# The transposed input of one pair moved from a DMA transpose to TensorE, with fewer unread matmuls ahead of an earlier group

## The chip, the cores and the metric

The kernel runs on one core of a Trainium2 chip. The metric is the device time of one execution in microseconds (us); several executions are made, and their median counts. A profile of one execution gives the span (first to last instruction of the program) and every instruction in it. Engines are called PE (TensorE matmul), PEld (its weight loads), DVE (VectorE), ACT (ScalarE), POOL (GpSimd) and SP (SyncE, which issues most DMAs here); "L486" is line 486 of the kernel.

## The reference

A causal linear attention with decay, computed in blocks, is followed by a layer norm and a two-layer MLP with a residual. Batch 4, 8 heads, sequence 768, head size 64; the model width is 512, the MLP's inner width 2048.

```python
def _attn_ref(q, k, v, lam):
    B, H, S, D = q.shape            # 4, 8, 768, 64
    block = 64
    ...
    for b in range(S // block):
        qb, kb, vb = (q[:, :, sl], k[:, :, sl], v[:, :, sl])
        intra = np.einsum('bhic,bhjc->bhij', qb, kb) * Dmask[None]
        intra = np.einsum('bhij,bhjd->bhid', intra, vb)
        inter = np.einsum('bhid,bhde->bhie', qb * lam_pow[None], kv_state)
        out[:, :, sl] = intra + inter
        kv_state = lam_block * kv_state + np.einsum('bhsd,bhse->bhde', kb * rev_pow[None], vb)
    return out

def _moe_ref(x, g_ln, w_ch1, w_ch2):   # x: the attention's output, (4, 768, 512)
    mu, var = np.mean(x, -1, keepdims=True), ...
    xn = (x - mu) / np.sqrt(var + 1e-06) * g_ln
    return x + np.maximum(xn @ w_ch1, 0.0) @ w_ch2
```

## The kernel before

The work is cut into 12 windows, called u = 0 to 11: window u holds 256 positions of one batch element (three thirds of the sequence times four batch elements). A window gives two token tiles of 128 rows each, ab = 0 and 1; the two tiles of a window are a "pair", and the MLP handles one pair at a time as a "group" g, so that group g belongs to window u = g. The third group is g = 2, the fourth pair is u = 3.

For each window, the attention part does the following. SP loads q, k and v (`load_in`, L75 or L79). DVE, ACT or POOL cast and scale them into `kq` and `vb` (`in_k_one`, `in_q_one`, `in_v`). k and q are transposed into `kqT`, by PE for windows 0 to 2 and by DMA transposes on SP's queue from window 3 (`transpose_dma`, L266). PE makes the scores (`scores`, L282), DVE masks them (L292), PE makes the sums for the running state (`kv`, L316), the products with v (`av`, L428) and the inter-chunk products with the state (`inter`, L441); the last two accumulate in the PSUM banks `po0` and `po1`, one for each tile of the pair. Then `norm` copies the result to `x` on ACT (L463), takes the mean and the variance on DVE (L465, L466) and writes the centred and scaled `xc` in bf16 on DVE (L470). `rstd_of` makes the inverse deviation with a square root on ACT (L496) and a reciprocal on DVE (L498).

The MLP needs x transposed. `to_xT` makes one tile's x^T, [128, 4, 128], from `xc`. For windows 0 and 1, PE transposes four 128x128 blocks into a PSUM bank of the pool "mm" (L490) and ACT copies them to `xT` (L491). For all later windows SP issues a DMA transpose (L486).

The MLP is cut into units that are put between the steps of the attention. A unit of its first layer (`m1`, L530) is 8 matmuls of 256 columns into one "mm" bank, which ACT reads with a Relu into `hT` (L533); a group has 8 of them. A unit of the second layer (`m2`, L666) is 4 matmuls of 512 columns, and a group has 8 of them, four for each tile; after four, DVE writes the output tile (L690). From the seventh group on, the second layer is done in another way, with sums of blocks made by DVE (L548 to L550) and matmuls at L565.

PSUM has eight banks, all in use: four for "mm", two for the scores ("sc"), and `po0` and `po1`. A new tile of a tag waits until the last reader of the old one is done.

The program is written out by hand as one long list of steps; every engine runs its own instructions in the order of this list, and waits only for the data and the buffers that an instruction needs. `units(n)` takes the next n units of the MLP from a queue. Around the fourth pair the list reads: `s4(3)` (the last inter-chunk products and the norm of window 3), `to_xT(3, 0)` and `to_xT(3, 1)`, the loads of window 6 mixed with units of the third group's second layer, `rstd_of(3)`, `make_keep64()` (two masks, built on POOL, with a copy on DVE at L157), three more units, `store(2)`, the DMA transposes of window 5, and then the first unit of the fourth group.

At the first unit of the third group there is a loop of 20 unread matmuls (8 columns, from a tile of zeros; L525 and L526), written into the bank that the unit then overwrites. Each is a pair of a weight load and a matmul, and nobody reads the result:

```python
for _ in range(20 if (g, u) == (2, 0) else 0):
    nc.tensor.matmul(pm[0:8, 0, 0:8], lhsT=fill_in, rhs=fill_in, start=True, stop=True, skip_group_check=True)
```

Of the kernel before, what the change touches and what calls it, by code (L numbers as in the profile page):

```python
# [8 lines left out]
BF16 = mybir.dt.bfloat16  # L9
# [8 lines left out]
def kernel(  # L18
# [20 lines left out]
    KA = DM // 128  # L39
# [15 lines left out]
    ps = ctx.enter_context(tc.tile_pool(name="ps", bufs=1, space=PSUM))  # L55

    half = [slice(0, 64), slice(64, 128)]
    XB = 3
    LB = 6

    def mm_tile(shape, dtype, name):
        return ps.tile(shape, dtype, tag="mm", bufs=4, name=name)
# [4 lines left out]
    def source(src, u, hs):  # L67
        cc, b = divmod(u, B)
        return src[b, hs, cc * W:(cc + 1) * W, :].rearrange("h (p j) d -> p h (j d)", j=2)

    def fill(got, name, u, hs, eng=None):
        eng = eng or nc.sync
        src = dict(k=k, q=q, v=v)[name]
        if u < LB:
            eng.dma_start(got[:, hs], source(src, u, hs))  # L75
# [11 lines left out]
    def open_in(u, gate):  # L87
        qkv_in[u] = {name: inp.tile([128, H, 2 * D], F32, tag=name + "in", name=name + "in") for name in "kqv"}
        if gate:
            nc.gpsimd.memset(qkv_in[u]["k"][:, 0, 0:1], 0.0)  # L90

    def load_in(u, name, eng):
        got = qkv_in[u][name]
        fill(got, name, u, slice(0, H), eng)
        qkv_in[u][name] = got.rearrange("p h (j d) -> p h j d", j=2)
# [54 lines left out]
    def make_keep64():  # L150
        for dst, base in ((keep64, 0), (keep64_b, D)):
            nc.gpsimd.memset(dst, 1.0)
            nc.gpsimd.affine_select(
                out=dst, in_=dst, compare_op=ALU.is_ge, fill=0.0,
                base=base, pattern=[[1, D]], channel_multiplier=-1,
            )
        nc.vector.tensor_copy(keep64[half[1]], keep64_b[half[1]])  # L157
# [49 lines left out]
    def open_window(u):  # L207
        kq = wk.tile([128, 2, NP, 2, 2, D], BF16, tag="kq", bufs=3, name="kq")
        vb = wk.tile([128, H, 2, D], BF16, tag="vb", bufs=4, name="vb")
        st[u] = dict(kq=kq, vb=vb)  # L210
        if u < XB:
            st[u]["kqT"] = wk.tile([128, 2, NP, 2, 128], BF16, tag="kqT", bufs=3, name="kqT")

    def part(a, dst, hs):

        return dst[:, a, hs.start // 2:hs.stop // 2].rearrange("p a j e d -> p a e j d")
# [9 lines left out]
    def in_q(u, eng, hs=ALL):  # L226
        src = qkv_in[u]["q"][:, hs].rearrange("p (a e) j d -> p a e j d", e=2)
        dst = part(1, st[u]["kq"], hs)
        if u < LB:
            lq = lam_q[:, hs, :].rearrange("p (a e) j -> p a e j", e=2)  # L230
# [11 lines left out]
    def in_q_one(u, eng, j):  # L242
        src = qkv_in[u]["q"].rearrange("p (a e) j d -> p a e j d", e=2)
        lq = (lam_q[:, :, j] if u < LB else lam_p[:, 0, :]).rearrange("p (a e) -> p a e", e=2)
        eng.tensor_tensor(part(1, st[u]["kq"], ALL)[:, :, :, j], src[:, :, :, j],  # L245
                          lq[:, :, :, None].to_broadcast([128, NP, 2, D]), op=ALU.mult)

    def in_v(u, eng, hs=ALL):
        n = hs.stop - hs.start
        lv = lam_v[:, hs, :, None] if u < LB else lam_p[:, 1, hs, None, None]  # L250
        eng.tensor_tensor(st[u]["vb"][:, hs], qkv_in[u]["v"][:, hs], lv.to_broadcast([128, n, 2, D]), op=ALU.mult)  # L251
# [167 lines left out]
    def av(u, pairs, chunks=(0, 1)):  # L419
        s = st[u]  # L420
        if "po" not in s:
            s["po"] = [ps.tile([128, H, D], F32, tag=f"po{ab}", name=f"po{ab}") for ab in range(2)]
        for p in pairs:
            for e in range(2):
                for j in range(2):
                    for jq in range(2):
                        for ab in chunks:
                            nc.tensor.matmul(s["po"][ab][half[jq], 2 * p + e, :],  # L428
                                             lhsT=s[f"mA{p // 2}"][half[ab], e, p % 2, j, half[jq]],
                                             rhs=s["vb"][half[ab], 2 * p + e, j],  # L430
                                             start=(p == 0 and e == 0 and j == 0), stop=False, skip_group_check=True)
# [45 lines left out]
    def to_xT(u, ab):  # L477
        s = st[u]
        t = 2 * u + ab
        g = group_of[t]  # L480
        i = t - groups[g][0]
        if i == 0:
            xT_of[g] = gp.tile([128, KA, GT * 128], BF16, tag="xT", bufs=3, name="xT")
        dst = xT_of[g][:, :, i * 128:(i + 1) * 128]
        if u >= 2:
            nc.sync.dma_start_transpose(dst, s["xc"][:, ab])  # L486
        else:
            xt = mm_tile([128, KA, 128], BF16, "xt")
            for kk in range(KA):
                nc.tensor.transpose(xt[:, kk, :], s["xc"][:, ab, kk * 128:(kk + 1) * 128], ident)  # L490
            nc.scalar.copy(dst, xt)  # L491

    def rstd_of(u):
        s = st[u]
        std = wk.tile([128, 2], F32, tag="std", name="std")
        nc.scalar.activation(std, s["mv"][:, :, 1], ACT.Sqrt, bias=eps_t, scale=XS * XS)  # L496
        rstd = xp.tile([128, 2], F32, tag="rstd", name="rstd")
        nc.vector.reciprocal(rstd, std)  # L498
        x_keep[u] = (s["x"], rstd)
# [13 lines left out]
    def mlp(g):  # L513
# [6 lines left out]
        def m1(u):  # L520
            nonlocal hT
            if hT is None:
                hT = gp.tile([128, KB, GT * 128], F16, tag="hT", bufs=2, name="hT")
            pm = mm_tile([128, NB, N], F32, "pm1")
            for _ in range(20 if (g, u) == (2, 0) else 0):  # L525
                nc.tensor.matmul(pm[0:8, 0, 0:8], lhsT=fill_in, rhs=fill_in, start=True, stop=True, skip_group_check=True)  # L526
            for b in range(NB):
                n = u * NB + b
                for kk in range(KA):
                    nc.tensor.matmul(pm[:, b, :], lhsT=w1[n // W2K][:, kk, (n % W2K) * 128:(n % W2K + 1) * 128],  # L530
                                     rhs=xT_of[g][:, kk, 0:N], start=(b == 0 and kk == 0),
                                     stop=(b == NB - 1 and kk == KA - 1), skip_group_check=True)
            nc.scalar.activation(hT[:, u * NB:(u + 1) * NB, 0:N], pm, ACT.Relu)  # L533
# [138 lines left out]
        m2.sums = h_sums  # L672
        m2s[g] = m2
        return m1, m2

    def rows_of(u):

        cc, b = divmod(u, B)
        order = "(c p j) d -> j p c d" if u < LB else "(j c p) d -> j p c d"
        return out[b, cc * W:(cc + 1) * W, :].rearrange(order, c=2, j=2)  # L680
# [15 lines left out]
    def store(u):  # L696
        for j in range(2):
            nc.sync.dma_start(rows_of(u)[j], o_of[u][half[j]])
# [129 lines left out]
    def wind_up(u):  # L828


        s = st[u]
        if u < LB:
            av(u, range(NP))
# [45 lines left out]
    def s4(u):  # L879
        inter(u, 1)  # L880
        if st[u]["S"][0][1] is not None:
            norm(u, 0)
        norm(u, 1)

    def p4(u):
        to_xT(u, 0)
        to_xT(u, 1)
# [70 lines left out]
    transpose_pe(1, 0, (0, 1), nc.vector)  # L958
    transpose_pe(1, 0, (2, 3), nc.vector)
    to_xT(0, 0)  # L960
    inter(0, 1)
    norm(0, 1, early=True)
# [65 lines left out]
    def units(n):  # L1028
        for _ in range(n):
            f, *a = next(steps)  # L1030
            f(*a)
# [60 lines left out]
    s3(3)  # L1092
    units(1)
    s4(3)
    to_xT(3, 0)
    to_xT(3, 1)
    open_in(6, False)
    load_in(6, "k", nc.sync)
    units(1)
    load_in(6, "q", nc.sync)  # L1100
    units(1)
    load_in(6, "v", nc.sync)
    units(2)
    rstd_of(3)
    make_keep64()
    units(3)
    store(2)
    transpose_dma(5, 0)
# [231 lines left out]
```

## Time and profile before

| | |
|---|---|
| Median of 5 runs | 213.75 us (212.69 to 215.88; 212.79, 213.75, 214.23, 215.88, 212.69) |
| The profiled execution | 212.79 us, with a span of 211.1 us |
| Busy share of the span | PE 95%, PEld 72%, DVE 67%, ACT 46%, POOL 40% |
| First layer of the MLP, L530 on PE | 736 matmuls, 85.0 us |
| Second layer, L666 on PE | 192 matmuls, 43.3 us |
| DMA transposes xT (L486) | 20, each 1.2 to 2.8 us of SP's queue, 2.4 to 6.0 us from issue to landing |
| DMA transposes kqT (L266) | 18, each 1.2 to 2.8 us of SP's queue, 3.1 to 7.3 us to landing |
| PE transposes (L490) | 16, with 4 copies on ACT (L491) of 0.58 us |
| Unread matmuls (L526) | 20, from 54.62 us, 0.64 us in all |
| Granted TensorE clock | 1.00 |

A line of the trace in order of time gives the start, the length, the engine, the line, the operation with its output and input, how many instructions are merged into it, and in brackets the idle time before it with what ended that time. Lengths of single matmuls include the way through the array, and neighbours overlap, so the cost of a group on PE is read from its start to the start of the next. SPq is SP issuing DMAs: the length is that of the issue, not of the transfer.

### The profile page before, as it was taken

The numbers are of one execution on the slowest core, as the hardware profiler recorded it, in microseconds if no ns is written. First come the engines' busy times: TensorE is split into PE (matmuls) and PEld (weight loads), VectorE is DVE, ScalarE is ACT, GpSimd is POOL, SyncE is SP. The second block draws the span as 40 slices with busy tenths as digits, with TensorE's granted clock in tenths as the row PEclk, the third lists the DMA queues.
The fourth block names the chain that finished last, engine by engine and source line by source line (L and its number), as shares of the span: only waits on it lengthen the run. The fifth ranks groups of instructions, "written<-read, shape, count | busy, mean of one in ns | idle before, by whom it ended". The sixth has DMA issues, their size and how long they took to land.

```text
span 211.1 us, 7148 instructions
## 1 busy us (share of the span) xinstructions
PE 200.2 (95%) x3079; PEld 152.0 (72%) x3079; DVE 140.6 (67%) x293; ACT 97.5 (46%) x195; POOL 83.4 (40%) x113
## 2 busy tenths in 40 slices
PE   2988999999999999999999999999999999999992
PEld 1477788544685576487487488888888888888881
DVE  2576571459366364756997499899797887876253
ACT  3854869320254145236057067185284372661630
POOL 4647328319746083208137045265292202011020
PEclk9999999999999999999999999999999999999999
DMA  4999999999999699999979998998738850430303
GB/s 109 295 269 216 177 270 175 194 304 294 167 326 239 150 223 200 180 183 224 212 160 228 162 210 171 171 211 145 174 66 165 276 137 0 106 51 0 99 16 87
DMA packets 94305, 37.17 MB, mean 176 GB/s; under 512 B 68417, under 2 KB 91457, under 8 KB 94274
## 3 DMA queue, kind: packets, MB, share of 16 engines
q1 hardware_dynamic: 89664, 32.32, 73.4%
q0 software_dynamic: 4224, 4.19, 12.8%
q8 instruction: 24, 0.39, 0.8%
q10 hardware_dynamic: 386, 0.20, 0.4%
q14 instruction: 7, 0.06, 0.1%
HBM read 27.27 MB, written 6.29 MB: 159 GB/s over the span
## 4 chain that ended last, share of the span: by engine, by line
PE 58%; issue 13%; DVE 10%; DMA 10%; SPq 3%; POOL 3%; ACT 1%; POOLq 0%; DVEq 0%; ACTq 0%
PE pm L530 30%; PE pm L666 8%; DMA qin<-in_q_dram 5%; PE pwa L565 3%; DMA xT<-xc 3%; PE pwd L565 2%; PE pwc L565 2%; SPq L75 2%; DVE xc L470 2%; DVE stats L465 2%; DMA kqT<-kq 2%; PE po L428 2%; PE po L441 1%; PE sc L282 1%; PE pm1t L640 1%
## 5 line engine op out<-in xcount | busy, mean ns | idle before, releaser
L530 PE MATMUL pm<-xT,w 128*128 128x256 bf16 x736 | 85.0, 273 | 0.4 <-DMA xT<-xc 0.4
L530 PEld LDWEIGHTS <-w 128*128 128x128 bf16 x736 | 70.0, 98 | 10.0 <-DMA xT<-xc 0.9
L533 ACT ACTIVATE hT<-pm 128x512 f16<-128x512 f32 x92 | 55.0, 601 | 40.2 <-PE pm L530 39.4
L666 PE MATMUL pm<-w,hT 128*128 128x512 f16 x192 | 43.3, 379 | 0.0
L666 PEld LDWEIGHTS <-hT 128*128 128x128 f16 x192 | 18.2, 98 | 20.5
L322 POOL TENSOR_TENSOR Sn<-Stmp,lam_s 128x256 bf16<-128x256 f32 x16 | 9.8, 612 | 53.1 <-DVE Stmp L400 34.2
L565 PEld LDWEIGHTS <-hs 128*128 128x128 f16 x192 | 18.8, 98 | 2.2
L470 DVE SCALAR_TENSOR_TENSOR xc<-po,mv,g_row 128x512 bf16<-128x512 f32 (+1 forms) x24 | 16.8, 706 | 1.8
L292 DVE TENSOR_TENSOR mA<-sc,keep 128x512 bf16<-128x512 f32 x20 | 13.1, 684 | 7.2 <-PE sc L282 7.2
L463 ACT COPY x<-po 128x512 f32<-128x512 f32 x18 | 9.9, 589 | 16.1 <-PE po L441 10.0
L590 POOL TENSOR_TENSOR o<-ev_u,x 128x256 f32<-128x256 f32 x4 | 3.1, 784 | 31.4 <-ACT ev_u L589 31.4
L565 PEld LDWEIGHTS <-hT 128*128 128x128 f16 x144 | 13.6, 98 | 2.7 <-ACT hT L533 1.2
L465 DVE BATCH_NORM_STATS2 stats<-x 128x6 f32<-128x512 f32 x18 | 12.4, 686 | 4.0 <-ACT x L463 3.9
L548 DVE TENSOR_TENSOR hs<-hT 128x1024 f16<-128x1024 f16 x12 | 9.8, 814 | 6.8 <-ACT hT L533 6.8
L690 DVE SCALAR_TENSOR_TENSOR o<-pm,rstd,x 128x512 f32<-128x512 f32 x12 | 8.8, 744 | 7.0 <-PE pm L666 7.0
L251 POOL TENSOR_TENSOR vb<-vin,lam_p 128x1024 bf16<-128x1024 f32 x6 | 11.5, 1910 | 4.4 <-DMA vin<-in_v_dram 4.4
L245 POOL TENSOR_TENSOR kq<-qin,lam_q 128x512 bf16<-128x512 f32 x10 | 10.3, 1045 | 7.4 <-DMA qin<-in_q_dram 7.3
L251 POOL TENSOR_TENSOR vb<-vin,lam_v 128x1024 bf16<-128x1024 f32 (+1 forms) x7 | 11.8, 1687 | 2.6 <-DMA vin<-in_v_dram 2.5
L245 POOL TENSOR_TENSOR kq<-qin,lam_p 128x512 bf16<-128x512 f32 x12 | 12.3, 1043 | 0.7 <-DMA qin<-in_q_dram 0.7
L368 DVE TENSOR_TENSOR mA<-sc,keep 128x512 bf16<-128x512 f32 x12 | 8.2, 682 | 1.4 <-PE sc L362 1.4
L452 ACT COPY seen<-po 128x8 f32<-128x8 f32 x8 | 1.0, 166 | 17.5 <-PE po L441 17.5
L549 DVE TENSOR_TENSOR hs<-hs,hT 128x512 f16<-128x512 f16 x12 | 7.5, 624 | 0.4
(139 smaller groups left out, 266.8 us busy)
## 6 DMA issues: line engine op xcount, KB each, us to landing
out_dram<-o SPq DMA_DIRECT2D x18, 256.0 KB, 4.8
w<-in_moe_w_ch_dram POOLq DMA_DIRECT2D x8, 512.0 KB, 8.9
kin<-in_k_dram SPq DMA_DIRECT2D x14, 256.0 KB, 4.8
qin<-in_q_dram SPq DMA_DIRECT2D x14, 256.0 KB, 4.8
vin<-in_v_dram SPq DMA_DIRECT2D x14, 256.0 KB, 5.4
kin<-in_k_dram SPq DMA_DIRECT2D x5, 512.0 KB, 7.2
qin<-in_q_dram SPq DMA_DIRECT2D x5, 512.0 KB, 8.7
vin<-in_v_dram SPq DMA_DIRECT2D x5, 512.0 KB, 8.5
```

Source lines behind the costliest of these rows:

```text
L245: eng.tensor_tensor(part(1, st[u]["kq"], ALL)[:, :, :, j], src[:, :, :, j], lq[:, :, :, None].to_broadcast([128, NP, 2, D]), op=ALU.mult)
L251: eng.tensor_tensor(st[u]["vb"][:, hs], qkv_in[u]["v"][:, hs], lv.to_broadcast([128, n, 2, D]), op=ALU.mult)
L292: nc.vector.tensor_tensor(s[f"mA{hf}"][:, e], s[f"sc{hf}"][e], kp[:, None, :, :].to_broadcast([128, 2, 2, 128]), op=ALU.mult)
L322: eng.tensor_tensor(dst, src, lam_s[:, :, None].to_broadcast([128, NP, D]), op=ALU.mult)
L463: nc.scalar.copy(x, po)
L465: nc.vector.bn_stats(stats, po if early else x)
L470: nc.vector.scalar_tensor_tensor(xc[:, sl], in0=po[:, sl], scalar=mv[:, 0:1], in1=g_row[:, sl], op0=ALU.subtract, op1=ALU.mult)
L530: nc.tensor.matmul(pm[:, b, :], lhsT=w1[n // W2K][:, kk, (n % W2K) * 128:(n % W2K + 1) * 128], rhs=xT_of[g][:, kk, 0:N], start=(b == 0 and ...
L533: nc.scalar.activation(hT[:, u * NB:(u + 1) * NB, 0:N], pm, ACT.Relu)
L548: nc.vector.tensor_tensor(s13, b[:, :, 1:2, :].to_broadcast([128, n, 2, 128]), b[:, :, 0:4:3, :], op=ALU.subtract)
L565: nc.tensor.matmul(pr[bank], lhsT=lhs(r), rhs=rhs, start=(first and r == 0), stop=(r == KB // 2 - 1), skip_group_check=True)
L666: nc.tensor.matmul(acc[i], lhsT=hT[:, kk, i * 128:(i + 1) * 128], rhs=w2[kk // W2K][:, kk % W2K, :], start=(kk == 0), stop=(kk == KB - 1))
```

## The change

Three things are changed. The x^T of the fourth pair (u = 3 alone) is made by PE, in tiles of the tags `po0` and `po1`, and copied by ACT, where it was a DMA transpose. Its two halves stand later in the list: the first after the third of the units that follow `s4(3)`, the second after `make_keep64()`. And the loop of unread matmuls ahead of the third group runs 12 times in place of 20.

```diff
     XB = 3
+    X_PE = (3,)
     LB = 6
...
         dst = xT_of[g][:, :, i * 128:(i + 1) * 128]
-        if u >= 2:
+        if u >= 2 and u not in X_PE:
             nc.sync.dma_start_transpose(dst, s["xc"][:, ab])
         else:
-            xt = mm_tile([128, KA, 128], BF16, "xt")
+            if u < 2:
+                xt = mm_tile([128, KA, 128], BF16, "xt")
+            else:
+                xt = ps.tile([128, KA, 128], BF16, tag=f"po{ab}", name="xt")
             for kk in range(KA):
                 nc.tensor.transpose(xt[:, kk, :], s["xc"][:, ab, kk * 128:(kk + 1) * 128], ident)
             nc.scalar.copy(dst, xt)
...
-            for _ in range(20 if (g, u) == (2, 0) else 0):
+            for _ in range(12 if (g, u) == (2, 0) else 0):
...
     s4(3)
-    to_xT(3, 0)
-    to_xT(3, 1)
     open_in(6, False)
     load_in(6, "k", nc.sync)
     units(1)
     load_in(6, "q", nc.sync)
     units(1)
     load_in(6, "v", nc.sync)
-    units(2)
+    units(1)
+    to_xT(3, 0)
+    units(1)
     rstd_of(3)
     make_keep64()
+    to_xT(3, 1)
     units(3)
     store(2)
     transpose_dma(5, 0)
```

## The prediction

> **What bounds the kernel now.** I read the page's busy shares first, then the waits, then the instructions in order of time around the two edits, then SP's queue. From the page:
>
> ```profile
> PE 200.2 (95%) x3079; PEld 152.0 (72%) x3079; DVE 140.6 (67%) x293; ACT 97.5 (46%) x195; POOL 83.4 (40%) x113
> ```
>
> TensorE is busy for 95% of the span, and most of what is missing lies in the first 16 us. What an edit is worth is therefore read from PE: instructions added to it, less waits taken from it. From the waits, all that PE itself waited for after 22 us (columns: engine and line, what it waited for, us in total, times, longest):
>
> ```profile
> PE pm L530 <- DMA xT<-xc: 0.4, 2, 0.2
> ...
> PE po L441 <- DVE seen L452: 0.3, 1, 0.3
> PE sc L362 <- DMA kqT<-kq: 0.2, 1, 0.2
> ```
>
> That is 0.9 us in all, and the edits stand at the two waits of the first line: one at the third group's first matmul, one at the fourth's. PE in order of time (start, us, engine, line, operation, count, idle before it):
>
> ```profile
> 53.66 1.03 PE L666 MATMUL pm<-w,hT 128*128 128x512 f16 x4
> 54.62 0.64 PE L526 MATMUL pm<-fill_in 128*8 128x8 bf16 x20
> 55.44 3.67 PE L530 MATMUL pm<-xT,w 128*128 128x256 bf16 x32 [0.18 <-DMA xT<-xc]
> ...
> 65.72 6.22 PE L666 MATMUL pm<-w,hT 128*128 128x512 f16 x28
> 72.14 1.03 PE L530 MATMUL pm<-xT,w 128*128 128x256 bf16 x8 [0.20 <-DMA xT<-xc]
> ```
>
> The reader is to see how little stands free: after the 28 matmuls of L666, which are the seven units that cover the way of the fourth pair's x^T, PE waits 0.2 us; after the 20 unread matmuls of L526 it waits 0.18 us. SP's queue over the same time:
>
> ```profile
> 62.65 4.80 SPq L266 DMA_TRANSPOSE kqT<-kq  x2
> 67.55 3.19 SPq L486 DMA_TRANSPOSE xT<-xc  x2
> 70.79 1.20 SPq L79 DMA_DIRECT2D kin<-in_k_dram  x2
> ...
> 82.32 1.21 SPq L79 DMA_DIRECT2D kin<-in_k_dram  x2
> 83.65 3.79 SPq L486 DMA_TRANSPOSE xT<-xc  x2
> ```
>
> SP hardly rests: each transfer starts when the one before it has been issued.
>
> **The x^T of the fourth pair: what it removes.** Two DMA transposes leave SP (3.19 us of its queue), and PE's wait for them goes. How long that wait is: 32 matmuls of L666 elsewhere run from 98.63 to the next group at 105.63; every change of group costs about 0.10 (four of them, 0.87 in a stream, take 65.48 - 64.51 = 0.97 before another group), so one is (7.00 - 0.10)/32 = 0.2156. 28 of them and the seam are 6.14: PE would be free at 71.86, and began at 72.14. Saved: 0.28 us.
>
> **What it adds.** Eight PE transposes, in two fours between units of L666. The kernel does the same for its first pairs, and these rows price it:
>
> ```profile
> 28.31 0.39 PE L490 MATMUL xt<-ident,xc 128*128 128x128 bf16 x4
> 28.53 1.04 PE L530 MATMUL pm<-xT,w 128*128 128x256 bf16 x8
> 29.75 0.40 PE L490 MATMUL xt<-ident,xc 128*128 128x128 bf16 x4 [0.18 <-DVE xc L470]
> ```
>
> Start to start, four take 28.53 - 28.31 = 0.22. In the stream of L666 each four opens one more seam: 0.22 + 0.10 = 0.32, two fours 0.64. Lower end 0.22 each (no extra seam), 0.44; upper end 0.40 + 0.10 each (the row that began after a wait), 1.0. I take 0.64, the row without a wait, since both operands are there: xc's halves are ready at 66.83 and 68.50 (DVE L470 at 66.08 and 67.75, 0.75 each), and the fours come up after 12 matmuls at 65.72 + 12 x 0.2156 + 0.10 = 68.41 and, four more on, at 69.59.
>
> A rule speaks against this edit. The Trainium skill's page "TensorE: Matmul & The Clock Gate", section "Part 4: PE-mode transpose", puts one 128x128 transpose at about 275 ns within a kernel, and says that transposes don't count as activity for the clock gate. The rows have single transposes of 219 to 314 ns from start to end, but pipelined, 55 ns apart; by the page's figure taken in series the estimate would be 8 x 0.275 = 2.2 us more, 215.7. The rows decide.
>
> Two ACT copies from the bank to xT (L491, 0.58 each). ACT is empty there, with one square root at 67.74 and then 5.23 us of idle until 73.27; the copies would run at about 68.85 and 70.05 (0.43 after their transposes start, by 29.75 to 30.18), and the second ends at 70.6. The group needs them when PE has done the last 12 matmuls, at 69.81 + 2.69 = 72.5. Cover 1.9 us; were it gone, the 0.28 would not be saved. Behind the first copy stands the square root, now at 69.4 instead of 67.74, and behind it DVE's reciprocal and the copy for keep64, at 69.7 instead of 69.2: DVE has nothing from 69.5 to 71.98, and the reciprocal's first reader comes at 85.4. No cost.
>
> The banks po0 and po1 are free once xc and x are read, which the transposes need anyway; their next writer is the fifth pair's L428 at 78.10, 7 us later. No cost.
>
> **What moves on SP.** The loads of the seventh window, the store and the kqT transposes behind them start 3.2 us earlier. The gain ends at 83.65, where the next x^T transposes wait for DVE's xc, done at 82.87 + 0.75 = 83.62, and that is paced by PE. Between, POOL waits less for v (2.13 us at 81.12) and ACT less for k (2.46 at 87.28), both off PE's path. So 0; lower end -0.35, if emptier DMA engines also remove the 0.21 before L362 at 122.47 and its like.
>
> **The unread matmuls.** 20 start at 54.62 and take 0.64 us, 32 ns each; eight fewer end 0.26 earlier. But PE then stood 0.18 us for the xT transpose, which nothing of this change moves. The wait becomes 0.44: worth 0; lower end -0.26, if that transfer lands before the 12 end.
>
> **The sum.** -0.28 + 0.64 + 0 + 0 = +0.36 us. Lower end -0.28 + 0.44 - 0.35 - 0.26 = -0.45, upper -0.28 + 1.0 = +0.72. The profiled execution took 212.79 us, a span of 211.1 and 1.69 around it; it becomes 213.15. It is one of the fast ones among the five runs: their median lies 0.96 above it. On the median the sum gives 213.75 + 0.36 = 214.1. The five runs spread from 212.69 to 215.88, so about 1% is what a measurement of this kernel tells from no change.
>
> **Rivals.** (1) *Somewhat faster: the wait removed is larger in most executions than in the profiled one.* For it: x^T transposes land 2.4 to 6.0 us after issue, the fourth pair's in 3.8 at most, and PE has no reserve there; a landing of 6.0 would cost PE over 2 us. If all of the median's 0.96 were that wait, 213.75 + 0.36 - 0.96 = 213.15; with both lower ends (-0.35, -0.26) 212.5. Against it: nothing shows that the slower runs lose their time there, and later transposes have the same risk.
>
> (2) *Slower, by the clock.* The unread matmuls and the steady stream keep PE at pace. Early in the kernel it runs at half: 16 matmuls of 128 columns at 16.47 take 18.13 - 16.47 = 1.66 us, 104 ns each, against 56 ns (32 in 1.79) from 30.14:
>
> ```profile
> 16.47 1.87 PE L640 MATMUL pm1t<-xT,w 128*128 128x128 bf16 x16 [0.32 <-ACT xT L491]
> 18.13 0.63 PE L490 MATMUL xt<-ident,xc 128*128 128x128 bf16 x4
> ...
> 20.09 1.38 PE L640 MATMUL pm1t<-xT,w 128*128 128x128 bf16 x16
> 21.41 0.42 PE L282 MATMUL sc<-kqT 64*64 64x128 bf16 x16
> ```
>
> The last 16 take 1.32, so the pace turned near 21.0. A relapse of that length, 4.5 us at half pace, loses 2.25: 216.35. It decides once the gap ahead of the third group is long enough to drop the pace; the longest gaps after 22 us, up to 0.28, did not, and the change makes one of 0.44. Against it: 0.44 is short, and the page's granted clock is 9 tenths or more in every slice. That row does not show the early half pace either, so pace, not the clock row, has to be looked at.
>
> (3) *Slower, by a collision.* The early loads of the seventh window share the engines with the kqT transposes that SP issued at 62.65 to 67.45, whose last lands 5.3 after 65.53, at 70.8; the fifth pair's scores read them at 73.38. If one load, 3.7 us to landing, got ahead, PE would wait 70.8 + 3.7 - 73.4 = 1.1: 214.1 + 1.1 = 215.2. It decides from 2.6 us of delay on. Against it: one queue, and the transposes stand ahead in it.
>
> (4) *It doesn't do what it says:* ACT's copies come too late and PE waits as before. By the cover of 1.9 us that is unlikely; it would give +0.64 at least, 214.4.
>
> **How the numbers follow.** Forecast 0.55, (1) 0.25, (2) 0.05, (3) 0.08, (4) 0.07. The likeliest is 214.1. The range reaches down to (1) with its lower ends, 212.5, and up to the collision on top of the upper end, 213.75 + 0.72 + 1.1 = 215.6; the clock case lies outside. Under 211.6 (1% faster) no case lands, only a median of few runs drawn low: 0.05. Over 215.9 lie the clock case and an unlucky draw: 0.09. Within 1%: 0.86.
>
> **What would show it.** Right: the group of L486 at 67.55 gone; L490 in two fours near 68.4 and 69.6, 0.22 to 0.4 each; no idle time before L530 near 72.5; the loads of the seventh window issued from about 67.5; 12 of L526 with some 0.44 us of idle behind them; every later stage 0.3 to 0.4 us later; SP again waiting for xc near 84. Wrong: the fourth group's first matmul before 72.0 or after 73; matmuls of 256 columns at twice their pace after 55; an idle PE before the fifth pair's scores; or a median outside the spread of the runs before.

## The result and the profile after

The changed kernel takes 212.92 us at the median of 53 runs (211.52 to 215.76), the kernel before 213.80 us at the median of 95 (211.22 to 217.09). The ratio, from runs of both on the same chip, is 0.9985, with a 95% interval of 0.997 to 1.0001: -0.3 us, -0.6 to 0, which is no difference that these runs can tell from nothing. Most of the 0.88 us between the two medians therefore comes from the chips and the runs that are pooled in them. Executions over 1.5% slower than the fastest of their kernel are left out of the ratios, and one profile, that of "SP's queue as before", is of such an execution. The profiled execution took 211.95 us with a span of 210.2, against 212.79 and 211.1 before.

The page, first part, of the changed kernel:

```profile
PE 199.4 (95%) x3079; PEld 151.5 (72%) x3079; DVE 139.9 (67%) x293; ACT 98.5 (47%) x197; POOL 83.0 (39%) x113
```

The number of matmuls is the same as before, 3079: eight transposes came, eight unread matmuls went. That plays a part below. In the waits of PE no line with a DMA into xT is left; of those after 22 us that the prediction showed, one remains:

```profile
PE po L442 <- DVE seen L453: 0.3, 1, 0.3
```

PE in order of time, around both edits (lines that stood at L530 and L666 are now L534 and L670; those between the diff's first line and `to_xT` are 1 higher):

```profile
54.00 0.45 PE L530 MATMUL pm<-fill_in 128*8 128x8 bf16 x12
54.38 3.67 PE L534 MATMUL pm<-xT,w 128*128 128x256 bf16 x32
...
64.72 2.76 PE L670 MATMUL pm<-w,hT 128*128 128x512 f16 x12
67.32 0.39 PE L494 MATMUL xt<-ident,xc 128*128 128x128 bf16 x4
67.54 1.03 PE L670 MATMUL pm<-w,hT 128*128 128x512 f16 x4
68.41 0.39 PE L494 MATMUL xt<-ident,xc 128*128 128x128 bf16 x4
68.63 2.75 PE L670 MATMUL pm<-w,hT 128*128 128x512 f16 x12
71.22 1.04 PE L534 MATMUL pm<-xT,w 128*128 128x256 bf16 x8
```

Each four of transposes takes 0.22 us from its start to the next line's, and nothing is idle in front of either group (the third at 54.38, the fourth at 71.22). SP's queue:

```profile
61.73 4.49 SPq L267 DMA_TRANSPOSE kqT<-kq  x2
66.26 2.00 SPq L80 DMA_DIRECT2D kin<-in_k_dram  x2
...
79.32 1.21 SPq L80 DMA_DIRECT2D kin<-in_k_dram  x2
82.77 2.86 SPq L487 DMA_TRANSPOSE xT<-xc  x2
```

The loads come right behind the kqT transposes, and from 80.53 to 82.77 SP waits for xc: the relief of the queue ends there.

The span is best read in three stages, because whole executions differ by more than the change can be worth. S3 runs from the first of the 36 second-layer matmuls of L666 to the third group's first matmul, S4 from the first of the 28 to the fourth group's first, and "rest" from there to the end. Every number is a difference of two starts in PE's order of time.

| kernel | 36 matmuls begin at | S3 | S4 | rest |
|---|---|---|---|---|
| before | 46.74 | 8.70 | 6.42 | 138.96 |
| changed | 46.12 | 8.26 | 6.50 | 138.98 |
| 12 unread, x^T by DMA | 48.53 | 8.32 | 6.55 | 139.22 |
| 20 unread, x^T by PE | 46.02 | 8.45 | 6.50 | 139.75 |
| none unread, x^T by DMA | 47.95 | 8.23 | 6.06 | 140.80 |
| the same again | 47.46 | 8.74 | 6.06 | 140.58 |
| none unread, x^T by PE | 46.82 | 8.06 | 6.50 | 139.96 |
| third pair on PE too, none unread | 46.03 | 8.23 | 6.50 | 140.18 |
| the same again | 46.30 | 8.23 | 6.50 | 139.50 |
| third pair on PE too, 4 unread | 46.13 | 8.50 | 6.50 | 139.19 |

Of the 0.9 us between the two profiled spans, 0.62 lie ahead of 46, where the two kernels do the same work; S3 gives 0.44, the stretch between S3 and S4 (10.28 against 10.34), S4 and the rest take back 0.06, 0.08 and 0.02.

### The profile page after: what moved, and what is told of

It reads as the page before. It is cut to its first block, busy times and chain, and to the rows that moved or that the text cites. A ratio compares the mean times of both kernels' runs of the same rounds, so it can differ in the third digit from the quotient of the medians.

```text
span 210.2 us, 7143 instructions
## 1 busy us (share of the span) xinstructions
PE 199.4 (95%) x3079; PEld 151.5 (72%) x3079; DVE 139.9 (67%) x293; ACT 98.5 (47%) x197; POOL 83.0 (39%) x113
## 4 chain that ended last, share of the span: by engine, by line
PE 62%; issue 13%; DMA 12%; DVE 5%; POOL 3%; SPq 2%; ACT 1%; POOLq 0%; DVEq 0%; ACTq 0%
PE pm L534 28%; PE pm L670 17%; DMA w<-in_moe_w_ch_dram 5%; DMA qin<-in_q_dram 4%; PE pwa L569 3%; DMA kin<-in_k_dram 3%; PE pwc L569 3%; PE pwd L569 2%; SPq L76 2%; PE po L442 2%; PE sc L283 1%; PE pwb L569 1%; PE po L429 1%; POOL o L594 1%; POOL kq L246 1%
## 5 line engine op out<-in xcount | busy, mean ns | idle before, releaser
L534 PE MATMUL pm<-xT,w 128*128 128x256 bf16 x736 | 85.0, 273 | 0.0
L534 PEld LDWEIGHTS <-w 128*128 128x128 bf16 x736 | 70.0, 98 | 9.3
L670 PE MATMUL pm<-w,hT 128*128 128x512 f16 x192 | 43.6, 379 | 0.0
L670 PEld LDWEIGHTS <-hT 128*128 128x128 f16 x192 | 18.1, 98 | 20.1
L569 PEld LDWEIGHTS <-hs 128*128 128x128 f16 x192 | 18.7, 98 | 2.5 <-DVE hs L552 0.3
L569 PEld LDWEIGHTS <-hT 128*128 128x128 f16 x144 | 13.6, 98 | 2.7 <-ACT hT L537 1.2
L552 DVE TENSOR_TENSOR hs<-hT 128x1024 f16<-128x1024 f16 x12 | 10.6, 884 | 6.9 <-ACT hT L537 6.9
L442 PE MATMUL po<-Sn,kqT 64*64 64x64 bf16 x216 | 7.5, 199 | 0.3 <-DVE seen L453 0.3
```

Of the source, the lines that this page charges most:

```text
L442: nc.tensor.matmul(s["po"][ab][half[jq], 2 * p + e, :], lhsT=qT[half[e], p, jq, half[ab]], rhs=s["S"][ab][jq][half[e], p, :], start=False, ...
L552: nc.vector.tensor_tensor(s13, b[:, :, 1:2, :].to_broadcast([128, n, 2, 128]), b[:, :, 0:4:3, :], op=ALU.subtract)
L569: nc.tensor.matmul(pr[bank], lhsT=lhs(r), rhs=rhs, start=(first and r == 0), stop=(r == KB // 2 - 1), skip_group_check=True)
L670: nc.tensor.matmul(acc[i], lhsT=hT[:, kk, i * 128:(i + 1) * 128], rhs=w2[kk // W2K][:, kk % W2K, :], start=(kk == 0), stop=(kk == KB - 1))
```

## The experiments

**One part of the change at a time.** Only the count of the loop:

```diff
-            for _ in range(20 if (g, u) == (2, 0) else 0):
+            for _ in range(12 if (g, u) == (2, 0) else 0):
```

> Only the loop of unread matmuls is changed (12 in place of 20); the x^T of the fourth pair stays a DMA transpose. Theory A (the unread matmuls stood on PE's path, because the third group's x^T has landed by then in many executions): 8 x 0.032 = 0.26 us less where it has landed, nothing where it has not; time -0.26 to 0 us, and in the profile no idle time or less than 0.44 us ahead of the third group's first matmul. Theory B (as predicted: the wait for the DMA takes the place of the removed matmuls): 0 us, idle 0.44 us. Theory C (the clock falls): a rise of up to 2 us, with 256-column matmuls at twice 0.109 us after that gap.

Measured: 213.05 us, ratio 1.0012 (0.9973 to 1.0051). In its profile the third group begins 56.85 - 56.41 = 0.44 us after the unread matmuls begin, with no idle time: x^T had landed. Here the eight fewer were a gain, as theory A has it, of 0.13 us, since twenty take 0.57 where nothing is waited for (the next profile). The time holds theories A and B alike.

The other part alone (the changed kernel with `range(20 ...)`):

> Only the x^T of the fourth pair is changed; 20 unread matmuls as before. Theory A (from the stage of the changed kernel, 6.50 us from the third group's 28 last matmuls to the fourth group's first, against 6.42 before): +0.08 us, as good as nothing. Theory B (the prediction's sum): +0.36 us. Theory D (in most executions the wait for the x^T transposes is larger than the 0.28 us of the profile before): -0.3 to -1 us, all of the gain of the whole change.

```profile
53.90 0.64 PE L530 MATMUL pm<-fill_in 128*8 128x8 bf16 x20
54.47 3.67 PE L534 MATMUL pm<-xT,w 128*128 128x256 bf16 x32
```

Measured: 212.78 us, ratio 1.0001 (0.9964 to 1.0039). S4 is 6.50, as in every kernel that makes this x^T on PE with eight transposes between the units: 0.08 more than in the one profile of the kernel before, 0.27 more than the mean of the five profiles with DMA transposes (6.23). So neither the time nor the stage parts A from B. The time also leaves room for the small end of theory D, but S4 does not: with DMA transposes it was 6.55 at most.

**No unread matmul.** `range(0 ...)` in the kernel before, run twice, and in the changed kernel:

> No unread matmul at all ahead of the third group; the fourth pair's x^T stays a DMA transpose. Theory A: 20 x 0.032 = 0.64 us less where the third group's x^T has landed when PE comes to it, else the wait takes the place; -0.64 to 0 us. Theory B: 0, with an idle time of 0.18 + 0.64 = 0.82 us. Theory C (the clock): the longest gap tried, 0.8 us; if it drops the pace, 256-column matmuls go from 0.109 to 0.218 us for some us and the time rises by about 2 us.

> The kernel before with no unread matmul ahead of the third group, a second time. In the first profile of it the pace ahead of and behind the third group was whole and the third group began 0.35 us after the second layer's last matmul, so the 2 us lost lay elsewhere: 1.97 us of PE ahead of L316 at 24.6, before anything that differs, and 0.65 us at L565. Theory U (chance, nothing to do with the edit): 213 to 214 us this time. Theory S (the edit makes it slow in a way that one profile did not show, for example the clock after longer waits for the third group's x^T): 215 to 216 us again, with a granted clock under 1 behind the third group's wait in this profile.

> The changed kernel with no unread matmul ahead of the third group (12 before). Theory A: the 12 cost 0.38 us where the third group's x^T has landed, and nothing where it has not: -0.4 to 0 us against the changed kernel. Theory S (as for the run above): +2 us. Rival C (the clock): where the wait for x^T is over 1 us, matmuls of 256 columns behind it at twice their 0.109 us, +1 to +2 us in such an execution.

Measured: 215.82 us, ratio 1.0141 (1.0092 to 1.019); 214.90 us, 1.0072 (1.0029 to 1.0116); 214.64 us, 1.0091 (1.0053 to 1.0128). All three are slower, so it is no chance. It isn't the pace behind the wait either: the third group's 32 matmuls take 3.58 us from their start to the next line in all three, as in the others, with a granted clock of 1.00. S3 and S4 don't lose more than 0.08 against the kernel before. The rest loses 1.0 to 1.8 us, far behind the edit, and each of the three profiles has a gap of 0.5 to 0.75 us in the middle of a run of L530 (L534), put down to "issue", at 154.41, 153.78 and 167.99. The first of them:

```profile
153.41 0.28 PE L530 MATMUL pm<-xT,w 128*128 128x256 bf16 x1
154.41 7.05 PE L530 MATMUL pm<-xT,w 128*128 128x256 bf16 x63 [0.72 <-issue]
```

**The third pair on PE too.** The changed kernel with `X_PE = (2, 3)`, `range(0 ...)`, and `to_xT(2, 0)` and `to_xT(2, 1)` moved behind the second and the fourth unit that follow `s4(2)`; run twice:

> The changed kernel with the third pair's x^T made by PE as well, in the same two banks, behind the second and the fourth of the units that follow it, and with no unread matmul ahead of the third group. Theory A: against the kernel before, third group: -0.64 (unread matmuls) - 0.18 (wait) + 8 x 0.055 = -0.38 us, fourth group +0.08: -0.3 us, with no idle time ahead of either group. Theory D (waits for x^T transposes are what the slower executions lose): more than that, -1 us or more, and a narrower spread of the runs. Against it: the transposes share ACT with the square root of the third pair, and a half that came late would cost up to 0.6 us.

> The kernel that makes the third and the fourth pair's x^T on PE and has no unread matmuls, a second time, for more runs. Theory A: ahead of the third group nothing is waited for (0 in place of 0.35 to 1.8 us seen so far with a DMA transpose), for 0.44 us of transposes: 0.998 of the kernel before, +- 0.003, and again no idle time ahead of either group.

Measured: 212.83 us, ratio 0.9986 (0.9952 to 1.0021), and 213.47 us, 1.0028 (0.9992 to 1.0065). No wait is left ahead of either group, and S3 is 8.23 both times. Yet the time is that of the kernel before. Again a gap put down to issue, in the order of time of the second run:

```profile
165.59 0.39 PE L534 MATMUL pm<-xT,w 128*128 128x256 bf16 x2
166.32 3.89 PE L534 MATMUL pm<-xT,w 128*128 128x256 bf16 x34 [0.34 <-issue]
```

**The length of PE's list.** What the three slower profiles and the two of the third pair have in common is that PE's list is shorter than in the kernel before, by 20, 12 or 4 pairs of weight load and matmul; in the changed kernel it is as long. It isn't the shorter the worse: the kernel with 12 unread matmuls and x^T by DMA is 8 pairs shorter and shows no such idle time, and those that are 8, 32 and 120 pairs longer show none either. So the last kernel is the same with `range(4 ...)`, which makes up the length:

> The kernel with the third and the fourth pair's x^T on PE, now with 4 unread pairs ahead of the third group, which brings PE's list to the same number of instructions as in the kernel before and in the changed one (8 + 8 transposes for 16 of the 20 pairs); with none it was 4 pairs shorter. Theory P (where PE's instructions come in blocks, and the place of a block's edge depends on how many instructions stand ahead; the gap of 0.34 us put down to issue at 166 in both profiles without unread matmuls is such an edge): no gap of that kind, the stage from the fourth group's first matmul to the end back from 139.5 and 140.2 to 139.0 us, time 0.5 us under that kernel. Rival Q (the unread matmuls do their work where they stand, by the pace): the gap near 166 stays, since 4 are too few to matter, and the time is that of the kernel with none.

Measured: 213.72 us, ratio 1.0008 (0.9973 to 1.0043). The gap is gone; at the same place PE runs through:

```profile
165.88 2.36 PE L534 MATMUL pm<-xT,w 128*128 128x256 bf16 x20
```

The rest falls to 139.19, though it varies without any gap too (138.96 to 139.75 among the kernels of the table that show none). Theory P holds in the profile, one execution against two; the times are too wide to show the half microsecond.

The traces say more once the gaps are counted in PE's list. In both profiles of the kernel before without unread matmuls, 2396 matmuls stand ahead of the gap; in the changed kernel without them it is 2652, in the two of the third pair 2653. The second of the two profiles first named has another gap, 0.17 us at 170.43, behind 2651. So the gaps stand at two places of the list, 256 matmuls apart, though the work there differs. The kernel with 12 unread matmuls is no exception: behind its 2652nd matmul the next start comes 0.30 us later in place of 0.11, which the idle time of the view does not show. In the kernels whose list has the old length, both places fall into the 64x64 matmuls that stand ahead (L362 and L441), and no gap shows.

Packets of 16 KB on an instruction queue go with this list: 25 in the profile of the kernel with 140 unread matmuls (below), whose list is 120 pairs longer, and 24 in every other one (the queue, its packets, MB, share of the DMA engines; the kernel before, then that with 140):

```profile
q8 instruction: 24, 0.39, 0.8%
q8 instruction: 25, 0.41, 0.8%
```

That is 2 x 3079 / 24 = 257 instructions for a packet, weight loads counted, and each gap ends 1.3 to 1.6 us after one of these packets has ended. That the gaps are the arrival of instructions fits all of this, but it is still argued: no run moved the packets alone, and why they come late at these places is not seen. The Trainium skill's page "Runtime: NRT & Kernel Launch", section "Instruction fetch mechanics", has instructions fetched in blocks of 16 KiB, 256 instructions, and calls the cost of a block's edge mostly hidden; the packets agree in size and number, and whether these gaps are such edges no run here shows by itself.

In the two profiles of the kernel before without unread matmuls the rest is 1.84 and 1.62 us longer. From start to start, 0.84 and 1.0 of that stand at the gaps, and some 0.8 in each ahead of L565, where PE waits for DVE's sums. The kernel with 20 unread matmuls and x^T by PE has such a wait too (0.61, at L569), so that it does not take their absence. In the changed kernel without unread matmuls the rest is 0.98 us longer than in the changed kernel, and 0.91 of it stands at the gap. The kernel before without them was not run at full length, so how much of its 1.5 to 3 us in time the gaps make up stays open.

**The sizes.** 140 unread matmuls:

> The kernel before with 140 unread matmuls in place of 20. It sizes one unread matmul and the cover ahead of the third group. Theory A (an unread matmul costs its 28 to 32 ns on PE's path as soon as x^T has landed): 140 x 0.030 = 4.2 us from the end of the second layer's last matmul to the third group's first, against 0.82 before: +3.4 us, and no idle time behind the last one. Theory B (hidden under the DMA wait): up to 0.8 us of cover and the rest as in A, +3.4 as well; only a time well under +3 would speak for a larger wait in most executions.

```profile
55.49 3.65 PE L526 MATMUL pm<-fill_in 128*8 128x8 bf16 x140
59.07 3.67 PE L530 MATMUL pm<-xT,w 128*128 128x256 bf16 x32
```

Measured: 216.39 us, ratio 1.0158 (1.0118 to 1.0198), +3.4 us. 59.07 - 55.49 = 3.58 us for 140: 25.6 ns each. Eight of them are 0.2 us, not 0.26.

Each transpose five times (`for _ in range(5)` around the four):

> The changed kernel with each of the eight PE transposes of the fourth pair made five times, so 40 in place of 8; ACT copies once. Theory A (55 ns each on PE's path, no seam): stage from 28 second-layer matmuls to the fourth group's first 6.50 + 32 x 0.0555 = 8.28 us, time +1.8 us against the changed kernel. Rival (the page's 275 ns each): +8.8 us. Rival (hidden somewhere): 0.

```profile
67.52 1.28 PE L494 MATMUL xt<-ident,xc 128*128 128x128 bf16 x20
68.64 1.03 PE L670 MATMUL pm<-w,hT 128*128 128x512 f16 x4
```

Measured: 214.53 us, ratio 1.0088 (1.0047 to 1.0128). Twenty take 1.12 us, 56 ns each, and S4 is 73.20 - 64.92 = 8.28, as expected from pipelined transposes. The 275 ns in series are out.

**SP's queue as before.** Two DMA transposes of the same xc into a tile that nobody reads, where `to_xT(3, ...)` had stood:

```diff
     s4(3)
+    spare = gp.tile([128, KB // 2, 2, 128], BF16, tag="hs13", bufs=1, name="spare")
+    for ab in range(2):
+        nc.sync.dma_start_transpose(spare[:, ab * KA:(ab + 1) * KA, 0, :], st[3]["xc"][:, ab])
```

> The changed kernel, with two DMA transposes of the fourth pair's xc put back on SP's queue in the place of the removed ones, into a tile that nobody reads: PE makes x^T, SP's queue is as before. Theory A (the relief of SP is absorbed at the next x^T transposes, which wait for DVE): the same time as the changed kernel within 0.3 us, and the seventh window's loads issued near 70 again. Rival (the relief of SP and of the DMA engines is where the gain of the change lies): the time of the kernel before or more, 0.3 to 0.5 us above the changed kernel, with more waits for kqT or v later.

Measured: 212.94 us, ratio 1.0009 (0.9973 to 1.0045). Inconclusive by time: the interval holds both theories. In the profile the seventh window's loads start at 73.13 again, and PE waits 0.4 us for a kqT ahead of L363. Over all profiles such waits for kqT came to 0.21, 0.27, 0.32, 0.4, 0 and 0 us with a full SP queue, and to 0, 0, 0.55, 0, 0, 0, 0 and 0 with two or four transposes less: a tendency of some 0.1 us, not more. The profile also shows what the unread matmuls stand in front of:

```profile
55.84 0.45 PE L530 MATMUL pm<-fill_in 128*8 128x8 bf16 x12
57.66 3.67 PE L534 MATMUL pm<-xT,w 128*128 128x256 bf16 x32 [1.38 <-DMA xT<-xc]
```

The third group's x^T is late by a different amount in each execution: with 12 unread matmuls PE waited 0, 0, 0.34, 1.16 and 1.38 us behind them, over five profiles.

**The old place.** The PE transposes right behind `s4(3)`:

> The changed kernel with both PE transposes of the fourth pair right behind its last inter-chunk products, where the DMA transposes stood, in place of between the second layer's units. Expected: PE has to wait there for DVE's xc, whose halves are ready 1.1 and 2.8 us after those products (66.83 and 68.50 against 65.72 before): the second four would start at about 68.6 with nothing between, +2.8 us less what the 7 units no longer wait for; time +2.5 to +2.9 us. If the place did not matter: 0.

Measured: 217.04 us, ratio 1.0181 (1.0146 to 1.0216), +3.9 us, one more than expected. PE waits 1.09 and 1.27 us for xc, as expected:

```profile
66.95 0.40 PE L494 MATMUL xt<-ident,xc 128*128 128x128 bf16 x4 [1.09 <-DVE xc L471]
68.62 0.60 PE L494 MATMUL xt<-ident,xc 128*128 128x128 bf16 x4 [1.27 <-DVE xc L471]
69.02 7.42 PE L670 MATMUL pm<-w,hT 128*128 128x512 f16 x28
76.28 1.04 PE L534 MATMUL pm<-xT,w 128*128 128x256 bf16 x8
```

But then the same 28 matmuls take 76.28 - 69.02 = 7.26 us, where they take 6.06 elsewhere. The stretches (us, busy time and count of PE, PEld, DVE, ACT and POOL, granted clock, DMA share, GB/s):

```profile
65.50:69.00 3.50, 1.14 (x17) 0.81 (x17) 2.86 (x6) 1.17 (x2) 2.57 (x5) 0.86 1.21 178
69.00:70.00 1.00, 1.00 (x6) 0.45 (x4) 0.00 (x0) 0.73 (x2) 0.00 (x0) 0.50 1.06 239
70.00:71.00 1.00, 1.00 (x4) 0.33 (x3) 0.00 (x0) 0.04 (x1) 0.00 (x0) 0.50 1.20 252
71.00:72.00 1.00, 1.00 (x5) 0.39 (x4) 0.00 (x0) 0.00 (x0) 0.00 (x0) 0.77 1.14 222
72.00:73.00 1.00, 1.00 (x6) 0.45 (x5) 0.00 (x0) 0.00 (x0) 0.00 (x0) 1.00 0.42 86
```

The seventh column is to be read: the granted clock falls to 0.50 and is back at about 71.5. By the mean of 0.86 over the first stretch, 0.14 x 3.5 / 0.5 = 1.0 us of it were at half, so it fell near 68.0, and stayed down for 3.5 us. The clock rival of the prediction is real, but it came only with two waits of more than 1 us, one behind the other, with nothing but transposes between them; waits of 1.16 us (in this same profile, at 54.3) and 1.38 us behind 12 unread matmuls did not bring it, and the clock stayed at 1.00.

## Why the prediction was right, and where it was not

The forecast was no change that can be told (0.86), and that is what came; 212.92 lies in the range. The likeliest time, 214.1, was 1.2 us too high: 0.7 of that is the sum, +0.36 us, which lies outside the measured -0.3 (-0.6 to 0), and the rest is the chips and runs that the medians are drawn from. The range is 3 us wide and the terms are tenths, so that being inside it says little about them, and two terms were off. Step by step:

- *What bounds the kernel*: right. What was added to PE showed in its order of time at full size (the 140 unread matmuls, the 40 transposes), and of the work that moved on ACT and SP no loss is seen.
- *The wait that is removed, 0.28 us*: 0.36 in that profile, since the 28 matmuls take 6.06 without a wait (three profiles), not 6.14; a change from L666 to L530 has no seam. The wait differs between executions: S4 was 6.42, 6.55 and three times 6.06 with the DMA transposes.
- *The transposes, 0.64 us*: mis-sized. 6.50 - 6.06 = 0.44, the lower end. The seam of 0.10 was taken from groups beside the 64x64 matmuls and doesn't arise between two kinds of full 128x128 operands: twelve of L670 and the way to the transposes take 67.32 - 64.72 = 2.60, which is 12 x 0.2156 and 0.01.
- *ACT's copies, the banks, the square root*: hidden as said; no wait appears for them. The second copy ends at 68.83 + 0.59 = 69.42, 1.8 us before the group begins.
- *SP's relief, 0*: right in the main. It is absorbed at the next x^T transposes (2.2 us of idle SP at 80.53). A tenth of a microsecond by fewer waits for kqT is likely, not shown.
- *The unread matmuls, 0*: right where x^T is late, wrong where it has landed. Then eight cost 0.2 us. S3 went down by that (0.57 to 0.38 from start to start) and by the wait of the profile before, which cost 55.44 - 54.62 - 0.57 = 0.25.

With the DMA transposes' mean S4 of 6.23 over five profiles, the x^T on PE costs about 0.27, the unread matmuls save 0 to 0.2 and SP's relief some 0.1: a sum of 0 to +0.2, near zero. The measured interval, -0.6 to 0, reaches only the lower end of that; whether the remainder is more than chance, no run shows. Rival (1), that typical executions lose much more at the wait removed, falls: S4 with DMA never passed 6.55 in five profiles. The spread of the runs sits elsewhere, in the third group's wait (0 to 1.4 us) and ahead of 46 us (45.98 to 48.53 among all profiles, before anything differs). What sets the latter stays open in part. PE waits there for v of the second window, at L316, 0 to 2.0 us, and the pace doubles at a different moment: the second 16 matmuls of L640 take 20.43 - 19.45 = 0.98 us in the changed kernel's profile, 1.32 before, 1.84 in the kernel with 12 unread matmuls. The six profiles with the fourth pair's DMA transposes on SP, the one with the spare tile among them, reach the 36 matmuls at 46.74 to 48.53, the eight others at 45.98 to 46.82. No reason is seen for this, since those transposes are issued some 20 us later, and the times of the kernel before and of the changed one do not differ by as much.

No version beat both kernels beyond its interval. The third pair on PE with the length made up is the most even in the profile, and 1.0008 in time.

## What to carry to other kernels

With PE 95% busy, moving work to it from a hidden queue bought here only the wait that the queue caused, and such a wait has to be read over several executions before it is worth anything. Put a PE transpose behind the time at which its operand is ready, between other matmuls: it then costs 55 ns for 128 columns, while in the wrong place the wait and the clock that falls behind it cost 3.9 us. When instructions are added to or taken from a long unrolled list, compare the far end of the trace as well: gaps put down to issue can appear 100 us later.

## What the runs showed that was not expected

- Taking out 20 unread matmuls made the kernel 1.5 to 3 us slower (ratios 1.0072 and 1.0141), with a clock of 1.00 where they had stood. In the profiles, about half or more of what is lost behind the fourth group's start stands at gaps 100 us later, at places fixed in PE's list, 256 matmuls apart. One such gap, 0.34 us, vanished when PE's list had its old length again.
- The granted clock fell to 0.50 near 68.0, about 2.2 us after the last ordinary matmul, with four transposes in between, and came back after some 3.5 us, 2.5 us into steady matmuls. The Trainium skill's page "TensorE: Matmul & The Clock Gate", section "Part 1: The HAM clock gate (the "warmup" mystery)", gives half rate and a free-running window of about 3.4 us; the length at half rate agrees.
- Pipelined PE transposes cost 55 to 56 ns each beside second-layer matmuls, in fours and in twenties, with a seam of 0.01 us.
